# Attention parts queued ahead of the weight tile in the first block, and KTS as the first of four copies

## The chip, the cores and the metric

The kernel runs on one core of a Trainium2 chip. The metric is the device time of one execution in microseconds (us). The core has five engines that this text names: PE (TensorE, matrix products), DVE (VectorE), ACT (ScalarE), POOL (GpSimd) and SP (SyncE, which here only issues transfers). Each works through its own queue in order.

## The reference

Three layers follow each other. The first is a gated linear attention with 4 batches, 8 heads, 768 positions and 48 channels; the other two are gated feed-forward layers on 3072 rows of 384 channels.

```python
f = 1.0 / (1.0 + np.exp(-f_logit))
for t in range(S):
    state = f[:, :, t, :, None] * state + np.einsum('bhd,bhe->bhde', k[:, :, t], v[:, :, t])
    y[:, :, t] = np.einsum('bhd,bhde->bhe', q[:, :, t], state)
...
x = np.ascontiguousarray(attn_out.transpose(0, 2, 1, 3)).reshape(B * S, H * D)
...
return ((x @ w_a) * (x @ w_b) @ w_out).astype(np.float32)
...
h = x @ w_in
g = h - np.tanh(h)
return (g @ w_out).astype(np.float32)
```

## The kernel before

**Attention.** The 768 positions are cut into 12 chunks of 64, and each chunk into two halves of the batches: 24 steps, numbered 0 to 23. A step (`attn_step`, line 282) is a Python generator of twelve parts, named by the letters of `PHASES`: F (sigmoid of the gate), P (scan PRE), R (PMS, its reciprocal D, scan R), K (products KH and RA), V (copies of the state ST to VS_A and VS_B), S (TensorE: scores `sc` and the transpose `pk` of KH), M (line 326 on: ScalarE copies RA to RB, then `sc` to RA and to RB with a triangular select on POOL after each, then `pk` to KTS), U (`uu`, the state's update from KTS), Y (`yy`, the output from RA and RB), E (ScalarE copies y and x), L (VectorE subtracts for their low parts) and D (transfers x<-y).

**Feed-forward.** The rows are cut into six blocks of 512, four steps each (`moe1`, line 474). For each of 12 slices of the hidden width, TensorE computes the groups `a` and `b` of 9 matmuls each, ScalarE copies `a` to `asb`, VectorE multiplies to `gf`, ScalarE rounds that to `gh` and the low part goes to `gl`; a group `y` follows one slice later. A product in float32 is three matmuls of high and low parts. `moe1` yields three times for each slice, after `a`, after `gf` and after `y`: 36 slots to a block. The second layer follows after the six blocks.

**Weights.** They arrive as raw words. `w_tick` (line 430) converts the next tile: three VectorE operations (lines 125 to 127) make `wc`, ScalarE copies it to the high part (`w_a`, `w_b`, `w_o`, line 137) and POOL subtracts for the low part (line 139). `w_fetch` then issues the next load from SP's queue. In the first block each slot converts one tile, until 36 are done; a tile made in slot g is used in slot g + 4.

**What sets the order.** The schedule is written out by hand: the queues hold the instructions in the order in which Python emits them. A prologue (`SEQ`, line 58) runs steps 0 to 3, which must be done before the first block, and the first parts of step 4; `x` in it is a warm-up matmul, `c` a conversion. Then the loop at line 544 takes slot after slot. The parts of the coming steps are `pulses`, a list of (slot, step, part); line 404 sets the slot. Steps 4 to 7 run in the first block, with M in slots 2, 11, 19 and 27, U two slots later, and Y one after U. Before, a slot emits `moe1`'s piece, then `w_tick`, then its pulses:

```python
            if jb == 0:
                w_tick(min(NW1, npro + slot + 1))
            ...
            while pulses and pulses[0][0] <= g:
                _, i, p = pulses.pop(0)
                pulse(i, p)
```

**Banks.** `sc`, `pk`, the two `uu` and `yy` take PSUM banks in turn (`att_bank`, line 159): over 6 banks in the prologue, 2 in the first block and 3 from the second block on (lines 157, 531, 550). With two, the five of a step alternate, so the first `uu` has the bank of `sc`, and waits until RA's and RB's copies have read it.

Of the kernel before, what the change touches and what calls it, by code (L numbers as in the profile page):

```python
# [13 lines left out]
ACTF = mybir.ActivationFunctionType  # L14
# [14 lines left out]
def tile_kernel(ctx: ExitStack, tc: tile.TileContext, q, k, v, f, w_a, w_b, w_out, w_in, w_out2, l_fkq, l_tv, l_v, l_w1, l_w2, out):  # L29
    nc = tc.nc  # L30
# [69 lines left out]
    def gelm_small(h, tmp, total):  # L100
        u, v1, v2, xu = (tmp(x) for x in ("u", "v1", "v2", "xu"))
        nc.scalar.activation(u, h, ACTF.Square, accum_out=total)  # L102
        nc.scalar.activation(v1, u, ACTF.Square, bias=bias1)  # L103
        nc.scalar.activation(v2, u, ACTF.Square, bias=bias2)  # L104
        nc.vector.scalar_tensor_tensor(xu, u, Q4, h, ALU.mult, ALU.mult)  # L105
        nc.vector.scalar_tensor_tensor(v1, v1, Q_Y1, xu, ALU.add, ALU.mult)  # L106
        nc.vector.scalar_tensor_tensor(v2, v2, Q_Y2, v1, ALU.add, ALU.mult)  # L107
        return v2
# [10 lines left out]
    def w_start(item):  # L119
        name, m, st = item  # L120
        c = stage.tile([128, DM], I32, tag="wc", name="wc", bufs=3)
        s3 = st.rearrange("p (n two) -> p n two", two=2)
        lo, hi = s3[:, :, 0], s3[:, :, 1]
        t = bank(rot["conv"], "cv").bitcast(I32)[:, 0:DM] if rot["conv"] is not None else c
        nc.vector.tensor_scalar(t, hi, 3, 0x3FFFFFF8, ALU.logical_shift_left, ALU.bitwise_and)  # L125
        nc.vector.scalar_tensor_tensor(t, hi, -1073741824, t, ALU.bitwise_and, ALU.bitwise_or)  # L126
        nc.vector.scalar_tensor_tensor(c, lo, 29, t, ALU.logical_shift_right, ALU.bitwise_or)  # L127
        return name, m, st, c.bitcast(F32)

    def w_finish(item):  # L130
        name, m, st, c = item
        if name in "abo":
            wt = wpool.tile([128, 2, DM], F32R, tag="w", name=f"w_{name}{m}")
            W[name, m] = (wt[:, 0], wt[:, 1])
        else:
            wt = st.bitcast(F32R).rearrange("p (h n) -> p h n", h=2)
        nc.scalar.activation(wt[:, 0], c, ACTF.Copy)
        eng = nc.gpsimd if name in "abo" else nc.vector
        eng.tensor_tensor(wt[:, 1], c, wt[:, 0].bitcast(F32), ALU.subtract)
        if name not in "abo":  # L140
            spilled.append((name, m, wt))

    def w_spill():
        name, m, wt = spilled.pop(0)
        nc.sync.dma_start(out=wsp[2 * m + "ip".index(name)], in_=wt.bitcast(F32))

    def w_fill(name, m):
        wt = wpool.tile([128, 2, DM], F32R, tag="w", name=f"w_{name}{m}")
        nc.sync.dma_start(out=wt.bitcast(F32), in_=wsp[2 * m + "ip".index(name)])
        W[name, m] = (wt[:, 0], wt[:, 1])  # L150
# [8 lines left out]
    def att_bank(name):  # L159
        rot["att"] = (rot["att"] + 1) % rot["n"]  # L160
        return bank(rot["att"], name)
# [5 lines left out]
    with tc.manual_schedule(), ExitStack() as p1:  # L167
# [73 lines left out]
        def load_t(i, sl):  # L241
            t = t_of(i)
            if i < PRO:
                nc.sync.dma_start(out=t[:, sl], in_=l_fkq[i, :, sl])
            else:
                for r0 in (0, 64):
                    nc.sync.dma_start(out=t[r0:r0 + D, sl], in_=l_fkq[i, r0:r0 + D, sl])

        def load_v(i):
            w = w_of(i)  # L250
            for ab, (vs, r0) in enumerate(((w.VS_A, 64), (w.VS_B, 0))):
                nc.sync.dma_start(out=vs[r0:r0 + 64], in_=l_v[i, ab])

        def load_tv(i):
            nc.sync.dma_start(out=tv_of(i), in_=l_tv[i])
# [26 lines left out]
        def attn_step(i):  # L282
# [20 lines left out]
            KH, RA, RB, KTS = w.KH, w.RA, w.RB, w.KTS  # L303
# [17 lines left out]
            pk = att_bank("pk")  # L321
            for j in range(NJ):
                nc.tensor.transpose(  # L323
                    pk[:, 128 * j:128 * (j + 1)], KH[:, 2 * j:2 * j + 2, :].rearrange("p u s -> p (u s)"), ident)
            yield
            nc.scalar.activation(RB[64:128], RA[64:128], ACTF.Copy)
            for r_, rows in ((RA, slice(64, 128)), (RB, slice(0, 64))):
                nc.scalar.activation(r_[rows], sc[rows], ACTF.Copy)
# [1 line left out]
                    out=r_[rows], in_=r_[rows], compare_op=ALU.is_ge, fill=0.0,  # L330
                    base=0, pattern=[[0, U], [1, CH]], channel_multiplier=-1,
                )
            nc.scalar.activation(KTS, pk, ACTF.Copy)
            yield
            uus = [att_bank(f"uu{bl}").rearrange("p (u s) -> p u s", s=CH) for bl in range(2)]
            for j in range(NJ):
# [56 lines left out]
        def flag(pr):  # L393
            nc.tensor.transpose(pr[0:1, 0:128], ru, ident)
            nc.vector.tensor_reduce(r2, pr[0:1, 0:128], mybir.AxisListType.X, ALU.min)
            nc.vector.tensor_scalar(okf, r2, 0.5, None, ALU.is_ge)

        gens = {i: attn_step(i) for i in range(NSTEP)}
        pulses = []
        for jb in range(1, NBLK):  # L400
# [8 lines left out]
        def pulse(i, p):  # L409
            assert phase[i] == p  # L410
            phase[i] += 1
            if i >= PRO and p == 0 and i + 1 < NSTEP:
                load_t(i + 1, slice(0, 3))
            if i >= PRO and PHASES[p] == "K" and i + 1 < NSTEP:
                load_tv(i + 1)
            next(gens[i], None)
            if i >= PRO and PHASES[p] == "Y" and i + 1 < NSTEP:
                load_v(i + 1)
# [11 lines left out]
        def w_tick(upto):  # L430
            while nconv[0] < upto and (loaded or half):
                if loaded:
                    half.append(w_start(loaded.pop(0)))
                    w_fetch()
                if len(half) > 1 or not loaded or half[0][0] in "abo":
                    w_finish(half.pop(0))
                nconv[0] += 1

        def w_fetch(n=3):
            while WQ and len(loaded) < (n if WQ[0][0] in "abo" else 1):  # L440
                loaded.append(w_load(WQ.pop(0)))
# [66 lines left out]
        for it in SEQ.split():  # L508
# [6 lines left out]
            elif it[0] == "l":  # L515
                i = int(it[2])
# [6 lines left out]
            else:  # L523
                i, p = int(it[1]), PHASES.index(it[0])
# [12 lines left out]
        def load_x2(o):  # L537
            t = xp.tile([128, 2, KT, 512], F32R, tag="x", name="x2")
            for hl in range(2):
                nc.sync.dma_start(out=t[:, hl].bitcast(F32), in_=xs[o][hl])  # L540
            return [t[:, hl] for hl in range(2)]

        done = False
        for g, jb in enumerate(moe1(None)):
            slot = g % SLOTS
            if jb == 0:
                w_tick(min(NW1, npro + slot + 1))
            else:
                if g == SLOTS:
                    rot.update(n=3, conv=None)  # L550
                if spilled:
                    w_spill()
                if (g + LEAD) % (SLOTS // 4) in CONV and jb < NBLK - 1 or (jb == NBLK - 1 and slot == 0):
                    w_tick(min(nconv[0] + 1, NW2 + 1))
# [3 lines that stand above are left out]
            if not pulses and not done:  # L558
                done = True
                nc.vector.tensor_reduce(r1, PMS.rearrange("p i u -> p (i u)"), mybir.AxisListType.X, ALU.min)  # L560
                nc.vector.tensor_scalar(r1, r1, P_MIN, None, ALU.is_ge)
            if jb == NBLK - 1:
                if slot == 2:
                    x2first.append(load_x2(0))
                elif slot > 2 and fills and len(fills) > 2 * MF2 + 3 - slot:
                    w_fill(*fills.pop(0))
# [37 lines left out]
        for i in range(NO * MF2 + LAG):  # L604
            g = None
            if i < NO * MF2:
# [8 lines left out]
                g = gelm_small(ph, lambda tag: gp2.tile([128, 512], F32, tag=tag, name=tag), usum[:, i:i + 1])  # L615
# [188 lines left out]
```

## Time and profile before

| | us |
|---|---|
| median of 3 runs (lowest to highest) | 980.62 (980.6 to 981.83) |
| the profiled execution | 981.35 |
| its span, first to last instruction | 979.4 |
| PE busy | 952.7 (97%) |
| DVE busy | 605.5 (62%) |
| ACT busy | 491.4 (50%) |
| POOL busy | 133.4 (14%) |

The profile is of one execution. Its span leaves out 1.95 us of the time of that execution. Busy shares are means over stages of different kinds: the prologue (0 to about 36 us), the first block (to about 139 us), the other five blocks of the first layer, and the second layer. A wait names the engine that stood still, its line, and what released it.

### The profile page before, as it was taken

What the parts mean: (1) busy time and instruction counts of PE and PEld (TensorE: products, weight loads), DVE (VectorE), ACT (ScalarE), POOL (GpSimd) and SP (SyncE); (2) the same over time, 40 slices, a digit from 0 to 9 for tenths busy, and PEclk for the clock granted to TensorE, in tenths of its full rate; (3) what the DMA queues carried; (4) which work ended last, traced back from release to release, by engine and by line L of the source; (5) the groups of instructions that cost most, each with busy time, mean ns of one, the idle gap of its engine ahead of it and who ended that gap; (6) DMA issues with size and microseconds to landing.
All of it is one profiled execution on the core that took longest, in us unless ns stands there. A gap on an engine that the chain in (4) does not pass through costs nothing.

```text
span 979.4 us, 15868 instructions
## 1 busy us (share of the span) xinstructions
PE 952.7 (97%) x6155; PEld 766.7 (78%) x6155; DVE 605.5 (62%) x1021; ACT 491.4 (50%) x949; POOL 133.4 (14%) x144
## 2 busy tenths in 40 slices
PE   7898899999999999999999999999999999999997
PEld 5677777878888878877888888888888888888885
DVE  6988866556666665565442257666666666666663
ACT  5544544344433444443321156666666666666663
POOL 6566651111111111111000000000000000000000
PEclk9999999999999999999999999999999999999999
DMA  9566656445534643472248650100100100200001
GB/s 284 134 185 172 185 125 192 113 108 179 145 108 125 195 124 109 141 196 85 76 159 291 192 180 1 63 35 1 65 33 1 65 33 16 82 0 1 33 1 35
DMA packets 41171, 104.53 MB, mean 107 GB/s; under 512 B 5600, under 2 KB 8672, under 8 KB 41088
## 3 DMA queue, kind: packets, MB, share of 16 engines
q1 hardware_dynamic: 40368, 102.45, 35.3%
q10 hardware_dynamic: 720, 0.98, 0.5%
q8 instruction: 50, 0.82, 0.4%
q14 instruction: 33, 0.27, 0.1%
HBM read 74.71 MB, written 26.74 MB: 104 GB/s over the span
## 4 chain that ended last, share of the span: by engine, by line
PE 88%; DVE 6%; issue 2%; ACT 2%; DMA 1%; SPq 0%; POOL 0%; DVEq 0%; ACTq 0%
PE o L165 20%; PE h L165 20%; PE b L165 14%; PE a L165 13%; PE y L165 13%; PE yy L358 2%; PE sc L319 2%; DVE cv L126 2%; PE uu L340 1%; DVE cv L125 1%; PE pk L323 1%; DVE wc L127 1%; DMA VS_B<-in_l_v_dram 1%; DVE R L299 1%; DVE gf L494 0%
## 5 line engine op out<-in xcount | busy, mean ns | idle before, releaser
L165 PE MATMUL h<-x,w_i 128*128 128x512 f32 x864 | 212.6, 391 | 0.0
L165 PE MATMUL o<-gh,w_p 128*128 128x512 f32 x576 | 195.1, 394 | 0.0
L165 PEld LDWEIGHTS h<-x,w_i 128*128 128x128 f32 x864 | 162.2, 188 | 36.1
L165 PE MATMUL a<-x,w_a 128*128 128x512 f32 x648 | 163.9, 397 | 2.6 <-ACT asb L489 2.3
L165 PE MATMUL b<-x,w_b 128*128 128x512 f32 x648 | 164.4, 398 | 0.0
L165 PE MATMUL y<-gh,w_o 128*128 128x512 f32 x432 | 148.0, 397 | 0.0
L165 PEld LDWEIGHTS a<-x,w_a 128*128 128x128 f32 x648 | 120.3, 188 | 30.4 <-ACT asb L489 2.7
L165 PEld LDWEIGHTS b<-x,w_b 128*128 128x128 f32 x648 | 119.9, 189 | 25.3
L105 DVE SCALAR_TENSOR_TENSOR xu<-u,h 128x512 f32<-128x512 f32 x96 | 66.0, 688 | 111.4 <-ACT u L102 111.2
L494 DVE TENSOR_TENSOR gf<-asb,b 128x512 f32<-128x512 f32 x72 | 49.3, 685 | 137.2 <-PE b L165 84.6
L165 PEld LDWEIGHTS o<-gh,w_p 128*128 128x128 f32 x576 | 108.1, 188 | 25.0 <-issue 0.2
L102 ACT ACTIVATE u<-h 128x512 f32<-128x512 f32 x96 | 57.4, 598 | 132.6 <-PE h L165 131.9
L165 PE MATMUL o<-gl,w_p 128*128 128x512 f32 x288 | 112.9, 392 | 0.0
L495 ACT ACTIVATE gh<-gf 128x512 fp32r<-128x512 f32 x72 | 45.5, 632 | 130.7 <-DVE gf L494 130.6
L489 ACT ACTIVATE asb<-a 128x512 f32<-128x512 f32 x72 | 42.9, 596 | 132.1 <-PE a L165 130.5
L165 PEld LDWEIGHTS y<-gh,w_o 128*128 128x128 f32 x432 | 81.8, 189 | 18.9
L165 PE MATMUL y<-gl,w_o 128*128 128x512 f32 x216 | 85.4, 395 | 0.0
L107 DVE SCALAR_TENSOR_TENSOR v<-v,v 128x512 f32<-128x512 f32 x96 | 66.5, 693 | 10.3 <-ACT gh L575 0.5
L106 DVE SCALAR_TENSOR_TENSOR v<-v,xu 128x512 f32<-128x512 f32 x96 | 66.5, 692 | 10.3 <-ACT v L103 0.5
L103 ACT ACTIVATE v<-u,bias 128x512 f32<-128x512 f32 x96 | 69.5, 724 | 3.1
L104 ACT ACTIVATE v<-u,bias 128x512 f32<-128x512 f32 x96 | 68.1, 709 | 0.6 <-DVE gl L576 0.6
L576 DVE TENSOR_TENSOR gl<-v,gh 128x512 fp32r<-128x512 f32 x96 | 65.7, 685 | 0.2 <-ACT gh L575 0.2
(95 smaller groups left out, 1114.4 us busy)
## 6 DMA issues: line engine op xcount, KB each, us to landing
wst<-in_l_w_dram SPq DMA_DIRECT2D x68, 384.0 KB, 3.3
wsp<-wst SPq DMA_DIRECT2D x32, 384.0 KB, 2.6
T<-in_l_fkq_dram SPq DMA_DIRECT2D x38, 288.0 KB, 5.4
x<-xs SPq DMA_DIRECT2D x12, 768.0 KB, 5.2
w_i<-wsp SPq DMA_DIRECT2D x16, 384.0 KB, 3.5
w_p<-wsp SPq DMA_DIRECT2D x16, 384.0 KB, 3.5
TV<-in_l_tv_dram SPq DMA_DIRECT2D x24, 192.0 KB, 2.8
xs<-oh SPq DMA_DIRECT2D x18, 256.0 KB, 2.3
```

The costliest lines, as they stand in the source:

```text
L102: nc.scalar.activation(u, h, ACTF.Square, accum_out=total)
L103: nc.scalar.activation(v1, u, ACTF.Square, bias=bias1)
L104: nc.scalar.activation(v2, u, ACTF.Square, bias=bias2)
L105: nc.vector.scalar_tensor_tensor(xu, u, Q4, h, ALU.mult, ALU.mult)
L106: nc.vector.scalar_tensor_tensor(v1, v1, Q_Y1, xu, ALU.add, ALU.mult)
L107: nc.vector.scalar_tensor_tensor(v2, v2, Q_Y2, v1, ALU.add, ALU.mult)
L126: nc.vector.scalar_tensor_tensor(t, hi, -1073741824, t, ALU.bitwise_and, ALU.bitwise_or)
L165: nc.tensor.matmul(dst, l_, r_, start=(first and i == 0), stop=(last and i == 2))
L489: nc.scalar.activation(asb, pb, ACTF.Copy)
L494: nc.vector.tensor_tensor(gf, asb, pab[1], ALU.mult)
L495: nc.scalar.activation(gh, gf, ACTF.Copy)
L576: nc.vector.tensor_tensor(gl, g, gh.bitcast(F32), ALU.subtract)
```

## The change

Two edits. In part M of a step, KTS is copied first instead of last. In the first block, a slot emits its pulses before `w_tick`; the loop over pulses further down then finds none left in that block, and other blocks keep their order.

```diff
--- before.py
+++ after.py
@@ -323,6 +323,7 @@
                 nc.tensor.transpose(
                     pk[:, 128 * j:128 * (j + 1)], KH[:, 2 * j:2 * j + 2, :].rearrange("p u s -> p (u s)"), ident)
             yield
+            nc.scalar.activation(KTS, pk, ACTF.Copy)
             nc.scalar.activation(RB[64:128], RA[64:128], ACTF.Copy)
             for r_, rows in ((RA, slice(64, 128)), (RB, slice(0, 64))):
                 nc.scalar.activation(r_[rows], sc[rows], ACTF.Copy)
@@ -330,7 +331,6 @@
                     out=r_[rows], in_=r_[rows], compare_op=ALU.is_ge, fill=0.0,
                     base=0, pattern=[[0, U], [1, CH]], channel_multiplier=-1,
                 )
-            nc.scalar.activation(KTS, pk, ACTF.Copy)
             yield
             uus = [att_bank(f"uu{bl}").rearrange("p (u s) -> p u s", s=CH) for bl in range(2)]
             for j in range(NJ):
@@ -544,6 +544,9 @@
         for g, jb in enumerate(moe1(None)):
             slot = g % SLOTS
             if jb == 0:
+                while pulses and pulses[0][0] <= g:
+                    _, i, p = pulses.pop(0)
+                    pulse(i, p)
                 w_tick(min(NW1, npro + slot + 1))
             else:
                 if g == SLOTS:
```

The order of the instructions on TensorE is the same row by row. On ScalarE, in the prologue (step 0, between the copies VX and the next step's sigmoid F), KTS moves ahead of RB, RA and RB:

```order
 L314 ACTIVATE VX<-VS_A 128x6x16
 L314 ACTIVATE VX<-VS_B 128x6x16
-L326 ACTIVATE RB<-RA 64x512
-L328 ACTIVATE RA<-sc 64x512
-L328 ACTIVATE RB<-sc 64x512
-L333 ACTIVATE KTS<-pk 128x512
+L326 ACTIVATE KTS<-pk 128x512
+L327 ACTIVATE RB<-RA 64x512
+L329 ACTIVATE RA<-sc 64x512
+L329 ACTIVATE RB<-sc 64x512
 L292 ACTIVATE F<-xt 128x8x64
 L350 ACTIVATE T_164<-uu_315 128x4x48
```

KTS needs `pk`, which follows `sc` on TensorE; the three copies that stood ahead of it are now behind it. The same holds in all 24 steps.

On ScalarE, in slots 0 to 3 of the first block (`asb` of slot 0 to `asb` of slot 3; `w_b`, `w_o`, `w_a` are the tiles of slots 0, 1 and 2), before:

```order
L489 ACTIVATE asb<-a 128x512
L137 ACTIVATE w_b_699<-wc 128x384
L310 ACTIVATE VS_A<-ST_130 64x8x48
L311 ACTIVATE VS_B<-ST_130 64x8x48
L495 ACTIVATE gh<-gf 128x512
L137 ACTIVATE w_o_727<-wc 128x384
L137 ACTIVATE w_a_737<-wc 128x384
L326 ACTIVATE RB<-RA 64x512
L328 ACTIVATE RA<-sc 64x512
L328 ACTIVATE RB<-sc 64x512
L333 ACTIVATE KTS<-pk 128x512
L489 ACTIVATE asb<-a 128x512
```

and now:

```order
L489 ACTIVATE asb<-a 128x512
L310 ACTIVATE VS_A<-ST_130 64x8x48
L311 ACTIVATE VS_B<-ST_130 64x8x48
L137 ACTIVATE w_b_701<-wc 128x384
L495 ACTIVATE gh<-gf 128x512
L137 ACTIVATE w_o_727<-wc 128x384
L326 ACTIVATE KTS<-pk 128x512
L327 ACTIVATE RB<-RA 64x512
L329 ACTIVATE RA<-sc 64x512
L329 ACTIVATE RB<-sc 64x512
L137 ACTIVATE w_a_765<-wc 128x384
L489 ACTIVATE asb<-a 128x512
```

The four copies of step 4 (slot 2) now stand ahead of the tile `w_a` of their slot, and VS_A, VS_B (slot 0) ahead of `w_b`. On VectorE, POOL and SP the parts of steps 4 to 7 move ahead of the slot's tile in the same way.

On ScalarE, at the end of the first block (slots 30 to 33; y and x are part E of step 7, `DMA` the three transfers of its part D, slot 32), before:

```order
L372 ACTIVATE y_882<-yy 128x128
L372 ACTIVATE x<-yy 128x3x128
L495 ACTIVATE gh<-gf 128x512
L137 ACTIVATE w_o_1715<-wc 128x384
L137 ACTIVATE w_o_1739<-wc 128x384
L381 DMA x<-y_882 16x2x512 x3
L489 ACTIVATE asb<-a 128x512
L495 ACTIVATE gh<-gf 128x512
```

and now:

```order
L372 ACTIVATE y_872<-yy 128x128
L372 ACTIVATE x<-yy 128x3x128
L137 ACTIVATE w_b_1691<-wc 128x384
L495 ACTIVATE gh<-gf 128x512
L137 ACTIVATE w_o_1720<-wc 128x384
L381 DMA x<-y_872 16x2x512 x3
L137 ACTIVATE w_o_1745<-wc 128x384
L489 ACTIVATE asb<-a 128x512
```

The three transfers now stand ahead of the last `w_o`, and y and x ahead of the `w_b` of their slot.

## Rows read from the trace of the kernel before

**Rows 1.** Windows: PE, PEld, DVE, ACT, POOL busy (x count), PEclk, DMA share, GB/s.
```profile
36.00:61.00 25.00, 20.89 (x174) 16.59 (x174) 22.10 (x41) 11.33 (x22) 14.12 (x14) 1.00 0.66 169
...
139.40:150.00 10.60, 10.60 (x97) 8.26 (x98) 4.52 (x7) 6.03 (x11) 2.60 (x3) 0.84 0.03 9
300.00:400.00 100.00, 100.00 (x855) 80.29 (x852) 57.04 (x105) 43.39 (x82) 14.67 (x15) 1.00 0.49 136
```

**Rows 2.** Waits, 37 to 140 us: us in total, times, longest.
```profile
PE uu L340 <- ACT KTS L333: 8.9, 4, 3.0
...
DVE gf L494 <- ACT asb L489: 3.7, 3, 1.7
DVE gf L494 <- PE b L165: 3.2, 2, 1.9
```

**Rows 3.** Timeline, ScalarE then VectorE, 45 to 51 us: start, us [idle before].
```profile
45.05 0.52 ACT L137 ACTIVATE w_o<-wc 128x384 fp32r<-128x384 f32 x1 [0.19 <-DVE wc L127]
46.90 0.52 ACT L137 ACTIVATE w_a<-wc 128x384 fp32r<-128x384 f32 x1 [1.32 <-DVE wc L127]
47.45 0.63 ACT L326 ACTIVATE RB<-RA 64x512 f32<-64x512 f32 x1
48.11 0.59 ACT L328 ACTIVATE RA<-sc 64x512 f32<-64x512 f32 x1
48.73 0.59 ACT L328 ACTIVATE RB<-sc 64x512 f32<-64x512 f32 x1
49.22 0.58 ACT L333 ACTIVATE KTS<-pk 128x512 f32<-128x512 f32 x1
49.70 0.58 ACT L489 ACTIVATE asb<-a 128x512 f32<-128x512 f32 x1
...
50.37 0.69 DVE L494 TENSOR_TENSOR gf<-asb,b 128x512 f32<-128x512 f32 x1 [1.65 <-ACT asb L489]
```

**Rows 4.** Timeline, TensorE, step 6 of the first block.
```profile
99.29 0.94 PE L340 MATMUL uu<-TV,KTS 64*64 64x48 f32 x32 [2.39 <-ACT KTS L333]
100.16 3.62 PE L165 MATMUL b<-x,w_b 128*128 128x512 f32 x9
```

**Rows 5.** Timeline, TensorE in the prologue; the last row from the chain.
```profile
10.47 1.11 PE L323 MATMUL pk<-ident,KH 128*128 128x128 f32 x4
13.87 0.37 PE L358 MATMUL yy<-RB,VS_B 128*64 128x64 f32 x1
...
27.39 0.27 PE L358 MATMUL yy<-RB,VS_B 128*64 128x64 f32 x1
...
30.33 0.66 PE L323 MATMUL pk<-ident,KH 128*128 128x128 f32 x4
...
33.43 0.27 PE yy L358 x4
```

**Rows 6.** Timeline, POOL: the select of RA, in step 1 and in step 4.
```profile
19.33 1.30 POOL L329 TENSOR_SCALAR_AFFINE_SELECT RA<-RA 64x512 f32<-64x512 f32 x1 [3.80 <-issue]
...
48.83 0.66 POOL L329 TENSOR_SCALAR_AFFINE_SELECT RA<-RA 64x512 f32<-64x512 f32 x1 [0.33 <-ACT RA L328]
```

**Rows 7.** Timeline, end of the first block: VectorE, ScalarE's queue, TensorE.
```profile
128.96 0.69 DVE L494 TENSOR_TENSOR gf<-asb,b 128x512 f32<-128x512 f32 x1 [1.36 <-PE b L165]
...
135.93 1.99 ACTq L381 DMA_DIRECT2D x<-y  x3
...
139.37 3.21 PE L165 MATMUL a<-x,w_a 128*128 128x512 f32 x9 [2.25 <-ACT asb L489]
157.12 2.20 PE L165 MATMUL a<-x,w_a 128*128 128x512 f32 x9
```

**Rows 8.** Timeline: VectorE's scan R twice, POOL beside the second.
```profile
36.88 1.24 DVE L299 TENSOR_TENSOR_SCAN R<-F,D 128x520 f32<-128x520 f32 x1
...
132.40 1.72 DVE L299 TENSOR_TENSOR_SCAN R<-F,D 128x520 f32<-128x520 f32 x1
...
132.01 1.01 POOL L139 TENSOR_TENSOR w_o<-wc,w_o 128x384 fp32r<-128x384 f32 x1 [0.32 <-ACT w_o L137]
```


## The prediction

> **What bounds the kernel now.** I read the windows by stage first. From 300 to 400 us TensorE is busy for all of 100 us: there the program is a single file of matmuls, and nothing on another engine shows in the time. From 36 to 61 us, in the first block, TensorE is busy for 20.89 us of 25 and VectorE for 22.10 [rows 1]. So everything that can be won or lost lies ahead of the second block, whose first group `a` starts at 139.37 us [rows 7]; what moves that start moves the end by as much.
>
> Second, the waits in the first block. VectorE stands still for 3.7 us behind ScalarE's copy `asb` (3 times) and for 3.2 us behind TensorE's group `b` (2 times): 6.9 us. TensorE waits 8.9 us for KTS, in 4 steps [rows 2]. VectorE's own row of work is long and in order, so I take it as the bound of this block: a TensorE wait counts only where VectorE then waits for TensorE.
>
> Third, why `asb` is late. ScalarE copies `w_o` at 45.05 us, then waits for VectorE to finish the next tile, copies it at 46.90 as `w_a`, and only then runs RB, RA, RB, KTS (47.45 to 49.80) and `asb` at 49.70 [rows 3]. VectorE, out of work at 48.72, starts `gf` at 50.37 after 1.65 us idle [rows 3].
>
> **The pulses ahead of the tile.** No instruction is added or removed; TensorE's order is the same row by row. ScalarE's four copies now stand before that `w_a`, so they start when `w_o` ends, at 45.57 instead of 47.45. The starts inside the group are 0.66, 0.62, 0.49 and 0.48 us apart [rows 3], 2.25 in all whatever their order, so `w_a` comes at 47.8, `asb` at 48.4 and ends at 49.0: `gf` starts at 49.0, not 50.37, and about 0.3 of the 1.65 us stays. The second step has the same shape. For each step in turn:
> - Steps 4 and 5: 1.65 us becomes 0.3, twice.
> - Step 6: `uu` starts at 99.29 after 2.39 us of waiting for KTS, and the `b` behind it takes 3.62 us [rows 4] against 2.20 for a group at full speed [rows 7]: TensorE came back from the wait at its lower level. In the new row the copies follow `gh` directly instead of waiting for a `w_o` conversion, so `uu` can start about 1.7 us sooner; VectorE's longest wait, 1.9 us, goes.
> - Step 7: the wait for `b` shrinks, but the copies now stand behind `asb` of their slot and `w_a`; I leave 0.4 us.
>
> That leaves 0.3 + 0.3 + 0.4 = 1.0 of 6.9 us: **5.9 us less**. The bounds are 6.9 (all of it) and 4.0 (if TensorE again returns slowly from its shorter waits, which costs 1.9 us once more).
>
> SP's queue moves too: T, TV, VS loads go one weight load forward. VS waits for `yy`, but weight loads wait for the tile's conversion, which ends later in the slot, so nothing queues behind VS; I cost it at nothing. If a VS load did hold one weight load back, VectorE would lose at most that one conversion's place, 1.85 us; the range has room for it. POOL's two selects now stand ahead of a weight subtraction, whose result is used four slots later: nothing.
>
> **The end of the first block.** ScalarE issues three x<-y transfers at 135.93, behind a `w_o` that had waited for its conversion, and `a` of the second block starts 3.44 us later, at 139.37 [rows 7]. Between the block's last `gf` but one (128.96 [rows 7]) and that issue stood two conversions beside y, x and R; with the new order it is one, as the issues precede the second tile. One conversion is 1.85 us, the distance of the copies that it releases at 45.05 and 46.90 [rows 3]. Against it, the last `y` group of the block needs the first of the two tiles, which y, x and R now delay, and keeps TensorE longer: I take **1.2 us less**, bounds 0 and 1.85. The wait of 2.25 us before this `a` falls to some tenths, and the granted clock, 0.84 on average from 139.4 to 150 us [rows 1], so partly at 1.2 GHz, should stay at 2.4: the group takes 2.20 instead of 3.21 us [rows 7]. **1.0 us less**, bounds 0 and 1.7 (0.16 of the 10.6 us of that stretch).
>
> **KTS first.** In the first block it buys nothing: `att_bank` turns over two banks there, and `uu`'s first bank is that of `sc`, which RA's and RB's copies read. `uu` waits for the last of the four copies, whichever it is.
>
> In the prologue it costs. There four steps (0 to 3) run as one chain: sc and pk on TensorE, ScalarE's copies, POOL's selects, `yy`, then the next step's sc. The RB copy used to run before or during sc, and RA needed only sc. Now all stand behind KTS, which needs pk. From the end of pk to the first `yy` that reads RB I count: 0.04 handover, 0.49 KTS, 0.66, 0.62 and 0.59 for the copies [rows 3], 0.1, a select of 0.66 [rows 6], 0.04: 3.20 us. Before, it was 13.87 - 11.58 = 2.29 us in step 0 and 33.43 - 30.99 = 2.44 us in step 3 [rows 5]; steps 1 and 2 lie between these. So 0.91 and 0.76 us, 0.83 on average, four times: 3.3 us later. `yy` of step 3 gives x to ScalarE and VectorE and so opens the first block; all of it passes on.
>
> The select can be longer: RA's took 1.30 us at 19.33, beside VectorE's scan, and 0.66 at 48.83 [rows 6]. I add one such case, 0.64: **4.0 us more**, bounds 0 (the delay hidden, see below) and 3.3 + 4 x 0.95 = 7.1 (both selects of each step lengthened).
>
> **A rule against it.** VectorE's scan R takes 1.72 us at 132.40, while POOL runs a subtraction from 132.01 to 133.02, and 1.24 us at 36.88 [rows 8]. The Trainium skill's page "SBUF — State Buffer", section "Who interferes with whom", says that a VectorE instruction with two SBUF inputs and a POOL instruction that reads SBUF share a port pair, and that the second to issue is fully blocked. By it R would lose the 0.62 us until POOL ends; the row shows 0.48, which agrees in kind. Each of the four steps has four such instructions (PRE, R, KH, RA). Which of them start behind POOL is drawn anew by the new order. I take as many as before, a cost of zero; the other draw is a rival.
>
> **Sum.** -5.9 - 1.2 - 1.0 + 4.0 = -4.1 us. The profiled execution took 981.35 us (span 979.4, and 1.95 around it), so 977.25; it lies 0.7 above the median of 980.62, and against that median the forecast is **976.5 us**. A measurement of this kernel can tell about 0.2%, 1.96 us, from no change: below 978.66 is faster, above 982.58 slower.
>
> **Rivals.**
> - Collisions take it back: a denser VectorE row starts more of its 16 instructions behind POOL. Three more selects lengthened in the prologue (3 x 0.64 = 1.9) and five more scans or products (5 x 0.48 = 2.4) cancel 4.1: about 980.8, no change. For it: VectorE has fewer gaps in which POOL can run. Against: the selects mostly fall into VectorE's waits in the prologue. This is the skill's port rule at work.
> - Slower, through the clock in the prologue: `yy` now waits longer behind `uu`. Waits of 2.39 and 2.25 us were followed by groups at the lower level [rows 4, 7]. From `yy`'s RB at 27.39 to pk's end at 30.99 TensorE works 3.6 us [rows 5]; at the lower level up to 3.6 more. It decides from two of three such stretches on: 7.2 - 4.1 = +3.1, 983.7 us; three give 987.3. Against: the new waits are some 1.9 us at most and broken by `yy` matmuls on RA, and pk already falls from 1.11 to 0.66 us within the prologue [rows 5], so the level is reached.
> - The prologue's delay is hidden: `uu` starts sooner with KTS first, and warm-up matmuls stand between; in step 3 `yy` came after a warm-up, not right after POOL. Then the 4.0 fall away: 972.5 us. Against: the sum of the pieces, 3.20 us, is longer than either of the two old ones shown.
> - The pulses do nothing, because VectorE only trades its waits for others further on. Then 4.0 are left, slower: 984.6. Against: the same instructions stand between each pair of `gf`, so there is nothing to trade for.
>
> **How the numbers follow.** The forecast has 0.56, with a range of its own of 974.0 to 978.6 (its bounds on prologue and clock). Collisions 0.22, at 978.7 to 982.5. Hidden delay 0.12. The two slower cases 0.10 together (clock 0.07, traded waits 0.03). Faster is 0.56 + 0.12 = 0.68, same 0.22, slower 0.10. The range of 972.8 to 981.2 leaves out the slower cases, the top of the collisions and half of the hidden delay.
>
> **What would show it.** Right: `yy` of step 3 starts at about 37, not 33.43, and the first `a` of the first block about 3.5 to 4 us later; VectorE's waits for `asb` and `b` fall from 6.9 to about 1 us; the second block's first `a` starts near 135 us and takes 2.2 us; after it nothing differs. `uu` still waits some 1 to 1.6 us per step in the first block, now for RB. Wrong: the prologue's `yy` not later, or pk at 1.11 us in steps 1 to 3, or VectorE's scans at 1.7 us more often than before, or VectorE's waits moved to another releaser.

## The result and the profile after

The changed kernel takes 991.63 us (median of 5 runs, 987.69 to 991.99); the kernel before, beside it on the same chip, 981.83 (980.6 to 982.11). The ratio is 1.0102 [1.0089, 1.0115]: **slower by 1%**, where 976.5 us was forecast. The profiled execution took 991.99 us, with a span of 990.2 against 979.4.

Where the time went is read from three marks. KH of step 4, the first work of the blocks on VectorE, starts at 47.12 us (before: 39.68), 7.44 later. The block's last `gf` but one comes 90.90 us behind it (before 89.28): 1.62 more. From there to the second block's first `a` it is 11.31 us (before 10.41): 0.90 more. That `a` then takes 4.11 us (before 3.21). The sum is 10.9 of the 10.8 us by which the span grew.

The same windows as in [rows 1], with its columns, after:

```profile
36.00:61.00 25.00, 22.43 (x240) 16.51 (x238) 20.88 (x34) 13.94 (x27) 14.85 (x16) 0.93 0.58 148
...
139.40:150.00 10.60, 6.65 (x23) 4.33 (x22) 9.98 (x15) 3.10 (x6) 5.07 (x5) 0.83 0.54 130
...
300.00:400.00 100.00, 100.00 (x782) 80.09 (x783) 62.42 (x117) 41.57 (x78) 11.73 (x12) 1.00 0.50 139
```

From 300 us on nothing differs. The stretch from 139.4 us is now still the end of the first block.

The waits after, 45 to 150 us, beside [rows 2]:

```profile
PE uu L340 <- ACT RB L329: 3.5, 4, 1.7
...
DVE gf L494 <- ACT asb L489: 0.7, 2, 0.4
```

VectorE's 6.9 us behind `asb` and `b` are down to 0.7, and TensorE's wait for KTS has become a shorter one for RB. That is as forecast, so the gain was made. It was spent on the same engine. VectorE's groups in the first block, before the change (38 to 140 us): busy time, mean in ns, then the idle time ahead and what ended it.

```profile
L494 DVE TENSOR_TENSOR gf<-asb,b 128x512 f32<-128x512 f32 x12 | 8.2, 682 | 8.5 <-ACT asb L489 3.7 <-PE b L165 3.2 <-POOL w_o L139 1.6
L299 DVE TENSOR_TENSOR_SCAN R<-F,D 128x520 f32<-128x520 f32 x5 | 7.2, 1435 | 0.2
L294 DVE TENSOR_TENSOR_SCAN PRE<-F,D 128x520 f32<-128x520 f32 x4 | 5.6, 1400 | 0.0
```

The same groups after (45 to 150 us):

```profile
L294 DVE TENSOR_TENSOR_SCAN PRE<-F,D 128x520 f32<-128x520 f32 x4 | 12.2, 3060 | 0.0
L494 DVE TENSOR_TENSOR gf<-asb,b 128x512 f32<-128x512 f32 x12 | 8.2, 683 | 0.9 <-ACT asb L489 0.7 <-issue 0.2
L299 DVE TENSOR_TENSOR_SCAN R<-F,D 128x520 f32<-128x520 f32 x5 | 8.1, 1612 | 0.2
```

The idle time ahead of `gf` falls by 7.6 us. The four PRE scans, the same instruction on the same data, take 6.6 us more: 3.06 us each in place of 1.40. It is a sign of being wrong that the prediction had named: of the nine scans in these groups seven take 1.7 us or more, before it was three. R takes 0.9 more. The busy column hides it: **an instruction that stands for a resource is booked as busy**, not as waiting.

The timeline after, at one of the long scans, VectorE's row first and then POOL's (start, us):

```profile
106.90 3.42 DVE L294 TENSOR_TENSOR_SCAN PRE<-F,D 128x520 f32<-128x520 f32 x1
...
105.82 0.66 POOL L330 TENSOR_SCALAR_AFFINE_SELECT RB<-RB 64x512 f32<-64x512 f32 x1
106.45 1.02 POOL L139 TENSOR_TENSOR w_o<-wc,w_o 128x384 fp32r<-128x384 f32 x1
107.43 1.00 POOL L139 TENSOR_TENSOR w_a<-wc,w_a 128x384 fp32r<-128x384 f32 x1
108.40 0.82 POOL L351 TENSOR_TENSOR ST<-T,PMS 128x384 f32<-128x384 f32 x1
```

The scan ends at 110.32 us, 1.10 after POOL's last instruction (109.22): about its own 1.23 us after the row. It stood through three POOL instructions, not one. The scans at 59.37 us (2.99) and 132.45 (3.94) end 1.11 us after a POOL row of the same kind, and so does the PRE ahead of the blocks, at 39.79 (2.81, before 1.70). Only the one at 84.49 took 1.90; there POOL had paused for 0.18 us just before.

Ahead of the blocks (compare [rows 5]), TensorE after:

```profile
20.25 0.66 PE L323 MATMUL pk<-ident,KH 128*128 128x128 f32 x4
...
21.59 0.68 PE L340 MATMUL uu<-TV,KTS 64*64 64x48 f32 x32 [0.47 <-ACT KTS L326]
23.65 0.48 PE L358 MATMUL yy<-RA,VS_A 128*64 128x64 f32 x2 [1.38 <-POOL RA L330]
...
24.36 0.37 PE L358 MATMUL yy<-RB,VS_B 128*64 128x64 f32 x1
...
27.05 0.39 PE L280 MATMUL warm<-wdum 128*128 128x512 bf16 x1
...
28.45 0.66 PE L323 MATMUL pk<-ident,KH 128*128 128x128 f32 x4
...
32.57 0.27 PE L358 MATMUL yy<-RB,VS_B 128*64 128x64 f32 x1 [0.27 <-POOL RB L330]
...
35.51 0.66 PE L323 MATMUL pk<-ident,KH 128*128 128x128 f32 x4
```

And windows of TensorE alone, after (length, busy, granted clock, DMA share, GB/s):

```profile
22.00:24.00 2.00, 0.62 (x23) 0.88 1.08 260
24.00:26.00 2.00, 1.98 (x34) 0.50 0.95 234
26.00:28.00 2.00, 2.00 (x41) 0.77 0.58 124
```

From pk's end to the first `yy` on RB it is 3.45 us in step 1 (20.91 to 24.36) and 3.46 in step 2, where before it was 2.29 to 2.44. And `yy` of step 1 runs at a granted clock of 0.50, the lower level of 1.2 GHz, after two waits; before, the clock was 1.00 in all three windows.

The timeline of the block's end, after, beside [rows 7]:

```profile
138.02 0.68 DVE L494 TENSOR_TENSOR gf<-asb,b 128x512 f32<-128x512 f32 x1
...
143.91 1.99 ACTq L381 DMA_DIRECT2D x<-y  x3
...
149.33 4.11 PE L165 MATMUL a<-x,w_a 128*128 128x512 f32 x9 [1.17 <-DMA wst<-in_l_w_dram]
```

The issue of x<-y came 5.89 us after that `gf`, before it was 6.97. But `a` followed the issue by 5.42 us, not 3.44.

### The profile page after: what moved, and what is told of

It reads as the page before. It is cut to its first block, busy times and chain, and to the rows that moved or that the text cites. A ratio compares the mean times of both kernels' runs of the same rounds, so it can differ in the third digit from the quotient of the medians.

```text
span 990.2 us, 15883 instructions
## 1 busy us (share of the span) xinstructions
PE 959.8 (97%) x6155; PEld 768.2 (78%) x6155; DVE 613.7 (62%) x1021; ACT 492.9 (50%) x949; POOL 128.6 (13%) x144
## 4 chain that ended last, share of the span: by engine, by line
PE 86%; DVE 8%; ACT 2%; issue 2%; DMA 1%; POOL 1%; DVEq 0%; SPq 0%; POOLq 0%
PE o L165 20%; PE h L165 20%; PE a L165 13%; PE y L165 13%; PE b L165 13%; PE yy L358 2%; PE sc L319 2%; DVE PRE L294 1%; DVE cv L126 1%; PE pk L323 1%; PE uu L340 1%; DVE cv L125 1%; DVE R L299 1%; DVE wc L127 1%; DMA T<-in_l_fkq_dram 1%
## 5 line engine op out<-in xcount | busy, mean ns | idle before, releaser
L165 PE MATMUL a<-x,w_a 128*128 128x512 f32 x648 | 167.0, 402 | 3.0 <-DVE x L375 1.3
```

Source lines behind the costliest of these rows:

```text
L165: nc.tensor.matmul(dst, l_, r_, start=(first and i == 0), stop=(last and i == 2))
```

## The experiments

The two edits were taken apart first. Each ratio is against the kernel before on the same chip; the chips differ between some of the versions. The cuts of code are against the changed kernel, if nothing else is said.

**Pulses ahead, KTS last.**

```diff
-            nc.scalar.activation(KTS, pk, ACTF.Copy)
             nc.scalar.activation(RB[64:128], RA[64:128], ACTF.Copy)
...
+            nc.scalar.activation(KTS, pk, ACTF.Copy)
```

> Only the pulses go ahead of the tile; KTS stays last. Theory: two faults add up in the changed kernel. KTS first makes the prologue some 7 us longer, and the pulses ahead of the tile pack POOL's work of a step into one row, behind which VectorE's scan PRE waits to the end of the row. Then the prologue is as before here (PRE of step 4 starts at about 33 us), VectorE's waits for asb fall below 1 us, but PRE of steps 5, 7 and 8 still takes about 3 us instead of 1.2 to 1.8: 983 to 986 us. Rival: the long scans come only from the shift that KTS first gives the block; then PRE takes 1.2 to 1.8 us and the time is about 976.

Measured: 978.04 us (10 runs), 0.9972 [0.9962, 0.9983]. Faster by 2.8 us, which is less than this edit's forecast terms (8.1). The four PRE scans take 1.87, 1.90, 1.51 and 2.01 us, longer than before by 1.7 us together, but not 3 each. So neither the theory nor the rival fits.

**KTS first, tile ahead.**

```diff
-                while pulses and pulses[0][0] <= g:
-                    _, i, p = pulses.pop(0)
-                    pulse(i, p)
                 w_tick(min(NW1, npro + slot + 1))
```

> Only KTS goes first; the tile stays ahead of the pulses. Theory: the first KH of step 4 comes at about 46 to 47 us instead of 39.7, and the first block then takes as long as before (KH of step 4 to the second block's first a: 99.7 us), PRE of steps 5 to 8 at 1.2 to 1.8 us: 988 to 989 us. Rival: the prologue's loss is due to the block's order, or is absorbed in the block: 982 or less.

Measured: 987.73 us (4 runs), 1.0071 [1.0051, 1.0092]. KH of step 4 starts at 47.38 us; the PRE scans of the block stay at 1.23 to 1.79. The theory held, within 0.4 us of its figures. So KTS first alone costs 6.8 us, ahead of the blocks. But -2.8 and +6.8 make +4.0, and both edits together gave +9.8: **some 6 us belong to neither edit alone.**

**Ahead only in the slots with a part M.**

```diff
-                while pulses and pulses[0][0] <= g:
+                while any(PHASES[e[2]] == "M" and e[0] <= g for e in pulses[:8]):
```

and KTS last.

> KTS last; only in the four slots with a part M do the pulses go ahead of the tile, so ScalarE's copies come early as in the changed kernel, while VectorE's own order is that of before. Theory: POOL's row is packed just as in the changed kernel, since ScalarE feeds it the same way, so PRE is still lengthened to 2 to 3 us in steps 5 to 7: 980 to 984 us. Rival: what lengthens PRE is VectorE's order (T and PRE ahead of the tile); then the waits for asb go (3.7 to about 0.7 us), PRE stays at 1.2 to 1.8 us, and the time is about 976 to 978.

Measured: 976.14 us (5 runs, 972.3 to 977.85), 0.9959 [0.9944, 0.9974]. The PRE scans take 1.36, 1.23, 1.23 and 1.24 us, so the rival held. The selects and copies can come early without a longer scan, if PRE stays behind the tile.

**The whole change with POOL's row thinned out.**

```diff
-        eng.tensor_tensor(wt[:, 1], c, wt[:, 0].bitcast(F32), ALU.subtract)
+        if name in "abo":
+            W[name, m] = (wt[:, 0], wt[:, 0])
+        else:
+            nc.vector.tensor_tensor(wt[:, 1], c, wt[:, 0].bitcast(F32), ALU.subtract)
```

> The changed kernel without POOL's subtraction for the low part of the first layer's weights (a, b and o); the matmuls read the high part in its place, so their number is the same. Theory: with those 36 instructions gone POOL has nothing in a row; PRE of steps 4 to 8 falls from 1.9 to 3.9 us to below 2.1 each, and the first block from KH of step 4 to the second block's first a shrinks from 102 to about 94 us: some 983 us. Rival: PRE waits for something else (its inputs, the clock); then it stays near 3 us and the time at about 991.

Measured: 978.14 us in a single run. From KH of step 4 to the second block's `a` it is 91.3 us against 102.2 with the whole change; PRE takes 1.90, 1.23, 1.23 and 1.44. The long scans are gone, as the theory has it. The four scans make up 6.4 of the 10.9 us, so the thinner row did more than free them.

**Which KTS makes the scans long?** Both edits, with KTS first in the blocks only, or ahead of them only.

```diff
-            nc.scalar.activation(KTS, pk, ACTF.Copy)
+            if i >= PRO:
+                nc.scalar.activation(KTS, pk, ACTF.Copy)
...
+            if i < PRO:
+                nc.scalar.activation(KTS, pk, ACTF.Copy)
```

> Both edits, but KTS is first only in the steps that run inside the blocks (step 4 on); the four steps ahead of the blocks keep KTS last. Theory (the long scans come from KTS being first inside the first block: it shifts POOL's selects so that POOL's row of instructions stands right in front of PRE): KH of step 4 starts at 39.5 to 40 us as before the change, the PRE scans of the first block take 2.5 us or more in the mean, and the time is 983 to 986. Rival (the long scans come from where the first block stands against the weight transfers and conversions after a later start): the PRE scans take 1.5 to 2.0 us each as with the parts alone moved, and the time is 977 to 979.5.

> The complement: both edits, but KTS is first only in the four steps ahead of the blocks, and last in the steps inside them. Theory (KTS inside the block makes the long scans): KH of step 4 starts at 47 us, the PRE scans of the first block take 2.0 us or less in the mean, and the time is the sum of the two edits alone, 983.5 to 986.5. Rival (the later start makes them): the PRE scans take 2.8 us or more in the mean and the time is 989 to 992, as with the whole change.

Measured: in the blocks only, 983.50 us (7 runs), 1.0028 [1.0015, 1.0041], with PRE at 2.98, 1.91, 3.42 and 3.92; ahead only, 984.63 us, 1.0042 [1.0025, 1.0059], with none of the four in the block above 2.03. (The profiled execution of the second took 988.62 us, the longest of its four.) The theory held both times, but for KH of step 4 in the first, which started at 40.44 us where 39.5 to 40 was expected. Against the version with the pulses alone KTS in the block costs 5.5 us, and the four scans took 4.9 more. The later start does nothing to them.

The timeline of the version with KTS first ahead of the blocks only, at the same place as above, VectorE and then POOL:

```profile
106.15 1.50 DVE L294 TENSOR_TENSOR_SCAN PRE<-F,D 128x520 f32<-128x520 f32 x1
...
104.89 0.65 POOL L331 TENSOR_SCALAR_AFFINE_SELECT RB<-RB 64x512 f32<-64x512 f32 x1
105.54 1.01 POOL L139 TENSOR_TENSOR w_o<-wc,w_o 128x384 fp32r<-128x384 f32 x1
106.51 1.94 POOL L139 TENSOR_TENSOR w_a<-wc,w_a 128x384 fp32r<-128x384 f32 x1
108.41 0.83 POOL L354 TENSOR_TENSOR ST<-T,PMS 128x384 f32<-128x384 f32 x1
```

The same instructions in the same order: here the scan waits for `w_o` alone, goes next, and it is `w_a` that is held (1.94 in place of 1.0). What is different is small: `w_o` starts 0.65 us after the select instead of 0.63, and does not overlap its end. With the pulses alone it is the same at this place: 0.65 us, and a scan of 1.51.

**A scan in a row of subtractions, alone.**

> Leaves the whole computation out and writes zeros: it only times one VectorE instruction (a scan over 520 elements with two inputs in SBUF; a product of two SBUF inputs over 512; the same with one input in PSUM) that is issued while POOL works through a row of one to four subtractions of 128x384, after two lengths of a small PSUM instruction ahead of it. Theory (the VectorE instruction stands until POOL's whole row is through): the scan ends about 1.1 us after the end of POOL's last instruction whatever the length of the row, so with four it takes over 4 us. Rival (it stands for the one POOL instruction under way and then goes ahead of the next): it takes at most 2.3 us in every row, and the next POOL instruction takes about 2.2. Both expect the one with a PSUM input to take under 0.8 us in every row.

The code repeats this for rows of one to four:

```
                    for j in range(n):
                        nc.gpsimd.tensor_tensor(lows[j], sb["C"][:, 0:384], sb["D"][:, 0:384], ALU.subtract)
...
                        nc.vector.tensor_tensor_scan(sb["SO"], sb["S1"], sb["S2"], 0.0, ALU.mult, ALU.add)
```

Measured: the rival held. The scan takes 1.23 or 1.79 us by its distance, the same for one and for four subtractions; the product with a PSUM input takes 0.69 throughout. So a long row is not enough, and the theory lacked a condition.

**The same at 25 distances, with and without a select at the row's head.**

> Leaves the whole computation out and writes zeros: POOL works through a row of four instructions that are all ready (four subtractions of 128x384; or a select, a subtraction of 128x512 and two of 128x384), and one VectorE scan of 520 elements is issued into the row, at 25 different distances from its start (VectorE instructions on PSUM ahead of it). Theory (a scan whose issue falls into the last few tenths of a microsecond of one POOL instruction finds the next one already started and stands to the end of the row): most scans take at most 2.3 us with the next POOL instruction lengthened to about 2, and those issued less than 0.15 us ahead of a POOL instruction's end take over 2.5 us. Rival (it depends on the kind of instruction ahead): the row of four subtractions never holds a scan for more than one instruction, and the mixed row does so whatever the distance.

In the row of four subtractions no scan takes over 2.01 us, at any distance. In the row with the select in front, every scan issued after the select's start ends about 1.1 us after POOL's last instruction: 4.86 us for the first of them, less by the distance for each later one, even when issued in the last of the four. So the theory, a moment close to an instruction's end, fell, and what is ahead in the row decides. The timeline with one of each, VectorE, then POOL (x2 and x4 are instructions in a row):

```profile
101.83 1.99 DVE L49 TENSOR_TENSOR_SCAN SO<-S,S 128x520 f32<-128x520 f32 x1
...
271.40 2.56 DVE L49 TENSOR_TENSOR_SCAN SO<-S,S 128x520 f32<-128x520 f32 x1
...
99.83 4.78 POOL L45 TENSOR_TENSOR low<-C,D 128x384 f32<-128x384 f32 x4
...
269.08 0.65 POOL L39 TENSOR_SCALAR_AFFINE_SELECT pre<-pre 64x512 f32<-64x512 f32 x1
269.71 1.25 POOL L43 TENSOR_TENSOR big<-C,D 128x512 f32<-128x512 f32 x1
270.93 1.93 POOL L45 TENSOR_TENSOR low<-C,D 128x384 f32<-128x384 f32 x2
```

The first scan is through at 103.82 us, before its row ends (104.61). The second, issued inside the last two subtractions, gets no turn between them and ends at 273.96, 1.10 after the row.

**Is it the select, and does a pause end it?**

> Leaves the whole computation out and writes zeros: rows of four POOL instructions (S a select, L a subtraction of 128x384, O a product with a constant, one input; G a subtraction that has to wait about 0.3 us for ScalarE), and one VectorE instruction issued at four distances into the row. Theory (the row is held from a select on, until POOL pauses): the scan ends about 1.1 us after POOL's last instruction in S-L-L-L, L-S-L-L and S-S-L-L, when it is issued behind the select; in S-G-L-L and in L-L-L-L it never takes over 2.1 us. If one input is what makes a select different, O-L-L-L is as S-L-L-L, if not as L-L-L-L. A product of two SBUF inputs in place of the scan is held as long by S-L-L-L, and one with a PSUM input takes 0.7 us throughout. Rival (the select is not the cause, the position in the row or the length of its instructions is): L-S-L-L and S-G-L-L don't differ from each other.

Measured (us that the VectorE instruction took at the four distances):

| row | took |
|---|---|
| S-L-L-L, scan | 2.56 (POOL was well into the row), 3.86, 3.12, 2.39 |
| S-S-L-L, scan | 1.72 (issued beside the first select), 3.56, 2.83, 2.10 |
| L-S-L-L, scan | 1.23, 1.46 (both issued before the select starts), 3.24, 2.51 |
| S-G-L-L (a pause after the select), scan | 1.72, 1.23, 1.72, 1.94 |
| O-L-L-L, scan | 1.70, 1.23, 2.07, 1.33 |
| L-L-L-L, scan | 1.23, 1.46, 1.67, 1.89 |
| S-L-L-L, product of two SBUF inputs | 4.04, 3.31, 2.58, 1.84 |
| S-L-L-L, product with a PSUM input | 0.69 four times |

The theory held in every row; one input is not what makes the select different. The 1.72 of S-S-L-L is a scan that got in between the two selects, which start 0.72 us apart and take 0.65: a pause of 0.07. The timeline of the row with a pause, VectorE and then POOL:

```profile
45.40 1.72 DVE L58 TENSOR_TENSOR_SCAN SO<-S,S 128x520 f32<-128x520 f32 x1
...
43.91 0.65 POOL L33 TENSOR_SCALAR_AFFINE_SELECT pre<-pre 64x512 f32<-64x512 f32 x1
45.03 0.99 POOL L36 TENSOR_TENSOR low<-C,g 128x384 f32<-128x384 f32 x1 [0.47 <-ACT g L45]
45.98 2.87 POOL L36 TENSOR_TENSOR low<-C,D 128x384 f32<-128x384 f32 x2
```

The scan waits for one subtraction and goes ahead of the next two (2.87 us in place of 1.93).

**A pause put back into the whole change.** A copy that nobody needs stands behind the four, where KTS was.

```diff
+            if i >= PRO:
+                nc.scalar.activation(wdum, KH.rearrange("p u s -> p (u s)"), ACTF.Copy)
             yield
```

> The whole change, and in the steps inside the blocks one more ScalarE copy of 512 columns (of KH, into a tile that nobody reads any more) behind the four, where KTS stood before: ScalarE's next work, the high half of a weight tile, comes 0.6 us later, so that POOL pauses between its second select and the subtraction behind it. Theory (a scan stands through POOL's whole row where the row begins with a select and has no pause since): in the first block the four PRE scans fall from 12.25 us together to 8 or less although more work was added, and the time falls by 4 to 6 from 991.63 to 985.5 to 988. Rival (the pause behind the selects has nothing to do with it, the scans are long because of what they meet in POOL's queue): the PRE scans stay at 11 us or more and the time at 991 to 994.

Measured: 985.13 us (5 runs), 1.0057 [1.0031, 1.0082]. That is 6.5 below the whole change, and 4.7 below it if each is set against the kernel before on its own chip, although work was added. Not all of it is the pause: in the profiled execution KH of step 4 starts at 45.70 us, 1.4 earlier, and up to there the two programs are alike. What the pause did is seen in the PRE scans: they take 1.85, 1.89, 1.71 and 1.57, 7.0 together in place of 12.2. The timeline of POOL around the first of them (it starts at 58.47 us):

```profile
54.20 0.65 POOL L330 TENSOR_SCALAR_AFFINE_SELECT RB<-RB 64x512 f32<-64x512 f32 x1
55.19 1.02 POOL L139 TENSOR_TENSOR w_a<-wc,w_a 128x384 fp32r<-128x384 f32 x1 [0.34 <-ACT w_a L137]
...
58.40 0.82 POOL L353 TENSOR_TENSOR ST<-T,PMS 128x384 f32<-128x384 f32 x1
59.19 1.94 POOL L139 TENSOR_TENSOR w_o<-wc,w_o 128x384 fp32r<-128x384 f32 x1
```

The row has 0.34 us of idle time on POOL that the whole change does not have, four instructions ahead, and the scan waits once and not to the end.

**TensorE kept busy ahead of the blocks.** Four warm-up matmuls between `uu` and `yy` of steps 0 to 2 (in the order string, `U1 Y1` becomes `U1 x x x x Y1`).

> The whole change, with four matmuls on a tile of zeros (as the program has them elsewhere) put into PE's queue between uu and yy of the first three steps, where PE waits 0.9 to 1.4 us for the selects. Theory (about 1.8 of the 7.4 us that the steps ahead of the blocks lost is TensorE at the lower of its clocks while it has such gaps): yy of the second step runs at full clock, KH of step 4 starts at 45.0 to 46.0 us in place of 47.12, and the time is 989.5 to 991, against 991.63 for the whole change. Rival (the clock lies off the path there, the copies and selects alone set the pace): KH of step 4 stays within 0.5 us of 47.12 and the time within 1 us.

Measured: KH of step 4 at 45.12 us, 2.0 earlier, and the granted clock 1.00 from 24 to 28 us. The median is 989.51 us (4 runs), 1.0088 [1.0057, 1.012]; that interval overlaps the whole change's, so the times do not show the 2 us. Nor does the trace show that these matmuls brought them. The version with POOL's row thinned out and the one with the pause have the same two waits in step 1 (0.47 and 1.38 us) and no matmuls in them, and their clock reads 1.00 from 22 to 28 us too (with the pause it was 0.50 from 16 to 18 us instead). So the theory's figures came out, but its cause stays open.

**The parts ahead in the slots with M or D, KTS last.**

(Against the version with M alone.)

```diff
-                while any(PHASES[e[2]] == "M" and e[0] <= g for e in pulses[:8]):
+                while any(PHASES[e[2]] in "MD" and e[0] <= g for e in pulses[:8]):
```

> KTS last; the parts go ahead of the weight tile only in the slots that hold a part M (the selects) or a part D (the transfers into X), in the other slots behind it. Theory (the transfers of X start 1.2 us earlier at the block's end and nothing else changes): 1 us below the version with M alone (976.14), 974.5 to 976, and the first a of the second block waits less than 1 us for a transfer. Rival (what comes ahead of the tile in the slots with D lengthens a scan or a weight tile by as much): 976 to 978.

Measured: 972.28 us (5 runs, 972.21 to 973.48), 0.9921 [0.9907, 0.9935]: better than expected, and faster than both kernels, than the one before by 8 us. VectorE's groups in its first block (38 to 135 us):

```profile
L494 DVE TENSOR_TENSOR gf<-asb,b 128x512 f32<-128x512 f32 x12 | 8.1, 679 | 3.1 <-PE b L165 2.0 <-ACT asb L489 1.1
...
L294 DVE TENSOR_TENSOR_SCAN PRE<-F,D 128x520 f32<-128x520 f32 x4 | 5.0, 1260 | 0.0
```

Two of its windows, with the columns of [rows 1]:

```profile
139.40:150.00 10.60, 10.60 (x103) 8.39 (x102) 7.19 (x14) 4.92 (x10) 1.62 (x1) 1.00 0.75 218
149.00:161.00 12.00, 12.00 (x83) 9.79 (x82) 8.34 (x16) 5.62 (x11) 0.66 (x1) 1.00 0.58 159
```

More idle time is left ahead of `gf` than with the change (3.1 against 0.9 us), but no scan is held, the second block's first `a` (133.04 us, 2.31 long) waits for nothing, and the clock stays at 1.00 where it fell to 0.84 before.

## Why the prediction was wrong

**The waits (-5.9): right.** 6.9 us became 0.7, and the mechanism, ScalarE's copies ahead of the tile, is the one described; `uu` waits for RB, as said.

**The collisions ("as many as before, a cost of zero"): this step failed.** They cost VectorE 8.5 us in the first block (PRE 6.6, R 0.9; the products RA 4.2 to 5.0 and KH 3.7 to 3.9). The rival on collisions had the right instructions and too small a price: 0.48 us each, from a scan that waited for the rest of one POOL instruction [rows 8]. A scan here lost up to 2.7 us, as it stood to the end of the row. The trace of before could not show that price: there ScalarE's KTS copy stood between the selects and its next work, and POOL paused for 0.29 to 0.77 us behind them in each step of the block.

This is also why "KTS first buys nothing in the first block" was only half of it. It bought nothing and **took away a pause**: without the copy behind RB, the high half of the next weight tile is ready when the second select ends, POOL goes on without a break, and with the pulses ahead PRE falls into that row. In the block either edit alone keeps the two apart.

The Trainium skill's page "SBUF — State Buffer", section "Who interferes with whom", says that a VectorE instruction with two SBUF inputs contends with a GpSimd instruction that reads SBUF, and, of VectorE's two-port modes, that whoever issues first gets the shared pair "for the whole instruction". A row of subtractions agrees (2.01 us at most for a scan of 1.23). A row with a select does not: the scan waited for up to three further instructions, 4.86 us. The section's rule that a VectorE instruction with at most one SBUF input, outside the two-port modes, does not contend agrees: 0.69 us in the rows with and without a select.

**The steps ahead of the blocks (+4.0): right in sign, 3.4 us too small.** Measured +7.44. Of it 5.18 us are there when pk of step 3 ends. Each step lost about 1.1 to 1.2 us, not 0.83 (3.45 us from pk to `yy`, where 3.20 was added up); three such steps make 3.4, and the start 0.1. The other 1.7 us TensorE lost in step 1: its `sc` took 1.82 us up to pk (18.43 to 20.25 us; before 1.28), and its `yy` took 2.69 up to the warm-up behind it (24.36 to 27.05; before 1.54). In that `yy` the granted clock was 0.50. This is the rival on the clock, for one stretch out of those it counted; in that `sc` the clock reads 1.00, so its 0.5 us stay unexplained. Against this rival the prediction had set that pk falls from 1.11 to 0.66 us, so that the level is reached; the granted clock reads 1.00 at both, so these lengths did not tell the level. Then the last step loses 1.3 us on ScalarE ahead of F (2.98 us from pk's end in place of 1.66) and 1.1 on a held PRE; no term stood for either (0.2 us came back behind it). No select was lengthened, for which the forecast had 0.64. The upper bound of 7.1 took 0.95 us a step for two lengthened selects, for which no row was given.

**The end of the block (-1.2) and the clock there (-1.0): lost.** The issue did come 1.1 us earlier after the last `gf` but one, as reasoned. But `a` came 2.0 us later after the issue, and no term stood for that. The last wait of `a` (1.17 us, after the last `y` had ended) is put down to a transfer. The one named is a weight load that `a` does not read; in five other versions the wait of this `a` is put down to x<-y. Those transfers took longer from issue to landing (last column, us), before and after:

```profile
x<-y ACTq DMA_DIRECT2D x3, 64.0 KB, 3.0
...
x<-y ACTq DMA_DIRECT2D x3, 64.0 KB, 4.8
```

The last `y` also waited 2.43 us for `w_o`, but that did not set the start of `a`. Seven of the versions have all parts ahead, and in each `a` follows the issue by 4.9 to 5.5 us, whether that `y` waited 2.4 us for `w_o` (three of them), about 0.5 or less (three) or not at all (the one with the thinner row). What slowed the transfers was not tested. In these seven SP issues a weight load of 384 KB less than 0.1 us ahead of them (4.2 to 4.9 us to landing). Where the tile stays ahead of part D (before, KTS first alone, M alone) the load is 1.0 to 1.1 us ahead (2.8 to 3.0 us), and with M or D it is 2.3 us behind (2.5 us).

`a` stayed slow (4.11 us): the granted clock was 0.50 from 147 to 153 us. A wait ahead of `a` does not do this by itself. With the pulses alone `a` waited 1.75 us and took 2.31 us at a clock of 1.00, as it did in the version with M or D, where it waited for nothing.

Term by term: 7.4 for 4.0, waits and collisions together about +1.6 for -5.9, the end +0.9 for -1.2, the clock +0.9 for -1.0.

## What to carry to other kernels

When two engines share something, count the queue behind the shared work, not only the instruction under way: a copy that looks like dead time on ScalarE was what left POOL a pause. Look for the cost in mean durations, since such standing is booked as busy. And test two edits apart and together: here -2.8 and +6.8 gave +9.8.

## What the runs showed of the hardware

- From a select on, a row of POOL instructions without a pause holds a VectorE scan or product of two SBUF inputs to the row's end (a scan ends 1.1 us after it, a product of 512 columns 0.56). Rows of subtractions, or with a one-input product at the head, let it in after one instruction (2.07 us at most). A pause of 0.07 to 0.47 us in the row ends the hold. In the kernel a start 0.02 us later seemed to be enough, in two versions; that was not tested by itself.
- Why a select does this is open; only this one (64x512) was tried, and no other POOL operation than the three named.
- After waits of 0.47 and 1.38 us in step 1 the granted clock of TensorE was 0.50 (24 to 26 us) in three versions (the whole change, KTS first with the tile ahead, KTS first ahead of the blocks only). It was 1.00 after the same two waits in two others, and one step later in all five. So these waits alone do not decide it.
